# One list order for a whole attention and MLP program, and half of its scores as three single-pass products

## The chip, the cores and the metric

The kernel runs on one core of a Trainium2 chip. The time is device microseconds of one execution on that core, from the start of the program to its end; runs are repeated and the median is given.

## The reference

Four images (B = 4) of 448 positions go through three stages, all in fp32:

```python
# 1. attention with a soft cap, 12 heads of 64
scores = cap * np.tanh(scale * q @ k.T / cap)
x = softmax(scores) @ v                       # -> (4, 448, 768)
# 2. experts: 4, each a causal attention with head size 64; a position uses its two best
for e in range(4):
    ye = softmax(causal(scale * (x @ wq[e]) @ (x @ wk[e]).T)) @ (x @ wv[e]) @ wo[e]
    out += w[e] * ye                          # w: softmax over the two best gates, else 0
# 3. gated MLP
h = gelu_tanh(out @ w_in)                     # 1024 wide
u, v = h[..., :512], h[..., 512:]
gated = u * (w_sg @ layer_norm(v) * g_ln + b_sg)
return out + gated @ w_out
```

## The kernel before, in words

The first stage works on 24 pairs of heads, six to an image, a pair's two heads on the two row halves of the array (64 partitions each). Scores are made with keys on the partitions: three blocks of 128 keys and a tail of 64 to a pair (`block`, L440, and `tails`, L446; one tail tile serves two pairs). A block is two fp32 products, one per head, of 64x128 weights with 448 columns. Each goes to a PSUM tile `s` of which there are two; ScalarE frees it by Tanh and then runs Exp on two blocks at a time (`scores`, L455). `add_up` (L481) adds the blocks for the softmax's sums on VectorE (some of these additions are GpSimd's), `sums` (L516) forms the sums over the keys on TensorE, and `values` (L487) multiplies with v, whose result `po` ScalarE copies to `os`. The inverse sums of an image go through DRAM (`rd`, `ri`, `rb`), then `os` is multiplied by them and split into two fp32r parts, xh and xl, for the experts.

The second stage makes its products as three fp32r products of two-part operands (high by high, high by low, low by high): `queries_keys` (L670, tile `qk`), values (`v`), the attention (`a`), transposes (`tr`, `turn`, L769) and `attend`. It runs for one image while the attention of the next goes on, and is spread over the slots.

Before the first image is done, TensorE also makes a combined weight w2 from wo and w_in (tiles `w2ps`, in `prepare_weights`, L941); its two parts go to DRAM, and four loads of 512 KB in slots 12 to 15 (`W2_LOADS`) bring them back for the MLP.

Three things set the order. The function `slot` (L550) is written out by hand: slot i holds pair i's scores, pair i - 1's values, the loads for pair i + 2, and at the places "a", "w", "p" and "n" pieces of the experts' work, of the weights and of the loads. Slots 0 to 9 are the program's first part, 10 to 24 its second. Engines keep the order in which the program is written (`InOrder`, L328), but loads and stores are placed by the tile framework. The rest, the last image's experts and the MLP, is the third part: there `agenda.on` is set, each instruction is recorded by `Agenda.add` (L103), and `Agenda.order` (L166) puts them into a list: of what is ready by a model of durations and buffers, the instruction with the longest way to the end (its level) goes first. SP's transfers are in that list too.

Of the kernel before, what the change touches and what calls it, by code (L numbers as in the profile page):

```python
# [22 lines left out]
HP = H // 2  # L23
# [54 lines left out]
class Agenda:  # L78
# [5 lines left out]
    def __init__(self, tc, since):  # L84
        self.tc, self.since = tc, since
        self.ops, self.on = [], False
        self.seen, self.uses, self.caps = {}, {}, {}
        self.behind, self.fill = {}, tuple(f"{t}{b}" for t in "ov" for b in range(B))
# [14 lines left out]
    def add(self, eng, f, args, kw):  # L103
# [9 lines left out]
        for x, wr in [(x, False) for x in ins] + [(x, True) for x in outs]:  # L113
            t = x.tensor
            lo, hi, p0, p1 = self.span(x)
            for j, l, h, q0, q1, w in self.seen.setdefault(t.name, []):
                if (wr or w) and lo < h and l < hi and p0 < q1 and q0 < p1 and j != i:
                    after.add(j)
            if t.name not in self.uses:
                self.uses[t.name] = []  # L120
                if x.space != bass.MemoryType.DRAM and getattr(t, "tag", None) is not None:
                    self.caps.setdefault(t.cap_key, []).append((t.name, wr, t))
            self.uses[t.name].append(i)
            tiles.append(t.name)
# [5 lines left out]
        op = dict(i=i, eng=eng, call=lambda: f(*args, **kw), after=after, tiles=set(tiles), took=[], port=False)  # L130
# [3 lines left out]
        if eng == "pe":  # L134
            st, mv = (args[1], args[1]) if name == "transpose" else (kw.get("lhsT", args[1]), kw.get("rhs", args[-1]))
            n = mv.free_size() if name != "transpose" else args[1].partition_size()
            op["dur"] = (96.0 if name == "transpose" else .446 * n + 3.5 if st.dtype == F32R else 2 * max(.825 * n, 185.0))
# [8 lines left out]
        elif eng == "dve":  # L146
            op["dur"] = 150.0 + 1.04 * n
            if name == "tensor_tensor_reduce":
                op["dur"] += 165.0
            elif name == "reciprocal":  # L150
                op["dur"] = 150.0 + 6.3 * n
            elif name in ("tensor_scalar", "tensor_copy") and not psum:
                op["dur"] = 150.0 + .54 * n + (110.0 if n > 8 and any(x.free_size() == 1 for x in ins) else 0.0)
            op["port"] = not psum and n > 8
        elif eng == "pool":
            op["dur"] = 100.0 + 2.4 * n if len(big) > 1 else 600.0 + .25 * n
            op["port"] = name != "memset"
        else:
            op["dur"] = 450.0
            size = outs[0].partition_size() * outs[0].free_size() * 4 if outs[0].space != bass.MemoryType.DRAM else (  # L160
                ins[0].partition_size() * ins[0].free_size() * 4)
            op["bytes"] = size
            op["extra"] = 1500.0 if outs[0].tensor.name.startswith(("rb", "ri", "rd", "wo", "gln")) else 0.0
        self.ops.append(op)

    def order(self):  # L166
        ops, n = self.ops, len(self.ops)
        then = [[] for _ in ops]
        for op in ops:
            for j in op["after"]:  # L170
                then[j].append(op["i"])
        level = [0.0] * n
        for i in reversed(range(n)):
            op = ops[i]
            took = op["dur"] + self.LATENCY[op["eng"]]
            if op["eng"] == "sp":
# [3 lines left out]
            level[i] = took + max((level[j] for j in then[i]), default=0.0)  # L180
        slots, queue, where, left = {}, {}, {}, {t: len(set(u)) for t, u in self.uses.items()}
        for key, tiles in self.caps.items():
            cap = tiles[0][2].tag_meta.bufs
            old = [t for t, w, _ in tiles if not w]
            slots[key] = [0.0] * (cap - len(old)) + [None] * len(old)
            queue[key] = [t for t, w, _ in tiles if w]
            for t, w, _ in tiles:
                where[t] = (key, len(slots[key]) - 1 - old.index(t) if not w else None)
        need, ready, end = [len(op["after"]) for op in ops], [0.0] * n, [0.0] * n
        for op in ops:  # L190
            for t in op["tiles"]:
                for k, v in self.since.items():
                    if t.startswith(k) and where.get(t, (0, 0))[1] is not None:
                        ready[op["i"]] = max(ready[op["i"]], v)
        open_ = {}
        for t, u in self.uses.items():
            made = {i for i in u if ops[i]["eng"] == "pe" and ops[i]["bank"] == t}
            open_[t] = {j for i in made for j in ops[i]["after"] if ops[j]["eng"] != "pe"} or ({-1} if not made else set())
        feeds = [[] for _ in ops]
        for t, js in open_.items():  # L200
            for j in js - {-1}:
                feeds[j].append(t)
        free = dict.fromkeys(self.LATENCY, 0.0)
        pools = {e: [] for e in free}
        for op in ops:
            if not need[op["i"]]:
                pools[op["eng"]].append(op["i"])
        grid, cfg, bank, lock, pipe, done = [[0.0] * 4 for _ in range(4)], None, None, 0.0, 0.0, []

        def begin(i):  # L210
            op = ops[i]
            t = max(free[op["eng"]], ready[i])
            for x in op["tiles"]:
                key, s = where.get(x, (None, 0))
                if s is not None:
                    continue
                if queue[key][0] != x and (not x.startswith(self.fill) or open_[x] or sum(s is not None for s in slots[key]) < 2):
                    return None
                got = [s for s in slots[key] if s is not None]
                if not got:  # L220
                    return None
                t = max(t, min(got) + 60.0)
            if op["eng"] == "pe":
                r, c, r0, c0 = op["cell"]
                if (r, c) != cfg and cfg:
                    t = max(t, max(map(max, grid)) + (95.0 if (r, c) != cfg else 0.0))
                else:
                    t = max(t, max(grid[y][x] for y in range(r0, r0 + r) for x in range(c0, c0 + c)))
            if op["port"]:
                t = max(t, lock)  # L230
            return t

        while len(done) < n:
            best = None
            for e, pool in pools.items():
# [6 lines left out]
                if e == "pe":  # L242
                    t, i = max(near, key=lambda x: (ops[x[1]]["bank"] == bank, level[x[1]], -x[1]))
                elif e == "sp":
                    t, i = min(near, key=lambda x: x[1])
                else:
                    t, i = max(near, key=lambda x: (level[x[1]], -x[1]))
                if best is None or t < best[0]:
# [6 lines left out]
            for x in op["tiles"]:  # L255
                key, s = where.get(x, (None, 0))
                if s is not None:
# [6 lines left out]
            if e == "pe":  # L264
# [4 lines left out]
                cfg, bank = (r, c), op["bank"]  # L269
                free[e], end[i] = t + 7.0, t + op["dur"]  # L270
            elif e == "sp":
                pipe = max(pipe, t + 1950.0) + op["bytes"] / 330.0
                free[e], end[i] = t + op["dur"], pipe + op["extra"]
            else:
                end[i] = t + op["dur"]
                free[e] = end[i] - self.OVERLAP[e]
                if op["port"]:
                    lock = max(lock, end[i] - 60.0)
            op["at"] = t
            done.append(i)  # L280
            for x in feeds[i]:
                open_[x].discard(i)
            for j in then[i]:
                lat = 0.0 if ops[j]["eng"] == e != "sp" else self.LATENCY[e]
                ready[j] = max(ready[j], end[i] + lat)
# [3 lines left out]
            for x in op["tiles"]:  # L289
                left[x] -= 1  # L290
                if not left[x] and x in where:
                    key, s = where[x]
                    slots[key][s] = max(end[j] for j in self.uses[x])
        return sorted(range(n), key=lambda i: (ops[i]["at"], i))

    def run(self):
        self.on = False
        last = {}
        for i in self.order():
            op = self.ops[i]  # L300
            ins = op["call"]()
            for key in op["took"]:
                before = last.get(key)
                if before is not None and before.ins.engine != ins.ins.engine:
                    self.tc.add_manual_dep(ins.ins, before.ins.name, NOSYNC, reason="order")
                last[key] = ins


def build(ctx: ExitStack, tc: tile.TileContext, a: dict):
# [35 lines left out]
    agenda = Agenda(tc, {"pe": 2300.0, "rd": 2700.0})  # L345
# [109 lines left out]
    def scores(b, hp, h, qp, kp, then=None):  # L455
# [4 lines left out]
        for c2 in range(n):  # L460
            s = ps_s.tile([128, 2, 512], F32, tag="s", name=f"s{b}_{hp}_{2 * h + c2}")
            if 2 * h + c2 < KB:
                block(s, 2 * h + c2, qp, kp)
# [86 lines left out]
    def slot(i, side):  # L550
# [6 lines left out]
        if i + 2 < len(pairs):  # L557
# [4 lines left out]
            ld[i + 2] = qk  # L562
        if i < len(pairs):
# [188 lines left out]
    def settle(b, ep):  # L752

        for el in range(2):
# [4 lines left out]
            for i in range(NC):  # L759
                pe = PES[b, ep, el, i]  # L760
                by = "apavaaap"[4 * el + i] if agenda.on else "p"
# [86 lines left out]
    W2_LOADS = (12, 13, 14, 15)  # L848
# [4 lines left out]
    def beside(n):  # L853
# [4 lines left out]
        def side(place):  # L858
# [10 lines left out]
            else:  # L869
# [135 lines left out]
    with tc.tile_pool(name="pre", bufs=2) as pre:  # L1005
# [13 lines left out]
    w2 = ES(tc.tile_pool(name="w2", bufs=1, reuse_waits="tile"))  # L1019
    w2_t = [w2.tile([128, 2, FF], F32R, name=f"w2_{t}") for t in "hl"]  # L1020
    w2_h, w2_l = w2_t
    YA = {}
    for n in range(PRE_SLOTS, B * HP + 1):
        slot(n, beside(n))
    ah.close()
    agenda.on = True
# [7 lines left out]
    ml = ES(tc.tile_pool(name="ml", bufs=1, side="right", reuse_waits="tile"))  # L1034
    ps = ES(tc.tile_pool(name="ps", bufs=5, space=PSUM, side="right", reuse_waits="tile"))
# [7 lines left out]
    wo_l = wp.tile([128, 2, DM], F32R, name="wo_l", tag="wb")  # L1043

# [3 lines left out]
    def mlp_weights(part):  # L1048
# [176 lines left out]
    agenda.run()  # L1225
# [56 lines left out]
```

## Time and profile before

| | us |
|---|---|
| median of 3 runs | 509.02 (508.78 to 509.1) |
| the profiled execution, its own time | 510.37 |
| its span, first to last instruction | 508.6 |
| TensorE busy, 2702 products | 496.8 (98%) |
| VectorE, ScalarE, GpSimd busy | 330.8, 329.0, 94.2 |

The span is cut into stages by what runs: scores alone to 20 us, scores with the preparation of weights to 100, scores with the experts of the image before to 265, the last experts and the first MLP work to 370, and the MLP to the end. A row's name is `out<-in` with the buffer numbers left out: `s<-qp,kp` is a score product of queries and keys, and w2_h and w2_l are printed as `w_h` and `w_l`. `x8` counts instructions; an fp32 product counts as two. All recorded operations share line L338, so tiles tell them apart. [...]

### The profile page before, as it was taken

The numbers are of one execution on the slowest core, as the hardware profiler recorded it, in microseconds if no ns is written. First come the engines' busy times: TensorE is split into PE (matmuls) and PEld (weight loads), VectorE is DVE, ScalarE is ACT, GpSimd is POOL, SyncE is SP. The second block draws the span as 40 slices with busy tenths as digits, with TensorE's granted clock in tenths as the row PEclk, the third lists the DMA queues.
The fourth block names the chain that finished last, engine by engine and source line by source line (L and its number), as shares of the span: only waits on it lengthen the run. The fifth ranks groups of instructions, "written<-read, shape, count | busy, mean of one in ns | idle before, by whom it ended". The sixth has DMA issues, their size and how long they took to land.

```text
span 508.6 us, 7515 instructions
## 1 busy us (share of the span) xinstructions
PE 496.8 (98%) x2702; PEld 329.6 (65%) x2702; DVE 330.8 (65%) x719; ACT 329.0 (65%) x558; POOL 94.2 (19%) x103
## 2 busy tenths in 40 slices
PE   7999999999999999999999989999999999999997
PEld 2233333455555556655559777877799899989996
DVE  4899998992666664655664999847860594497050
ACT  6989989868788686678765757757831263355131
POOL 0000000133145152235063302031410010010000
PEclk9999999999999999999999999999999999999999
DMA  8974626885334142414023622015011001100212
GB/s 292 310 267 141 216 88 141 241 295 176 102 102 151 58 129 63 127 58 113 1 68 88 193 60 64 1 46 233 1 37 54 19 1 56 54 0 1 90 43 85
DMA packets 35188, 54.27 MB, mean 107 GB/s; under 512 B 5584, under 2 KB 30160, under 8 KB 35152
## 3 DMA queue, kind: packets, MB, share of 16 engines
q1 hardware_dynamic: 35008, 53.57, 33.4%
q8 instruction: 21, 0.34, 0.3%
q10 hardware_dynamic: 144, 0.23, 0.2%
q14 instruction: 15, 0.12, 0.1%
HBM read 42.04 MB, written 11.75 MB: 106 GB/s over the span
## 4 chain that ended last, share of the span: by engine, by line
PE 72%; DVE 12%; ACT 7%; DMA 4%; SPq 2%; issue 2%; POOL 0%; DVEq 0%; ACTq 0%; POOLq 0%
PE o L338 17%; PE s L338 8%; PE qk L338 8%; PE po L338 8%; PE sp L338 7%; PE v L338 6%; ACT p L338 4%; PE hu L338 3%; DVE pb L338 3%; PE a L338 3%; PE av L338 3%; PE tr L338 2%; DMA rb<-rd 2%; PE hv L338 2%; ACT pe L338 2%
## 5 line engine op out<-in xcount | busy, mean ns | idle before, releaser
L338 ACT ACTIVATE p<-s,tsc 128x896 f32<-128x896 f32 x84 | 80.9, 1006 | 20.3 <-PE s L338 20.0
L338 PE MATMUL s<-qp,kp 64*128 64x448 f32 (+1 forms) x384 | 79.1, 573 | 3.0 <-ACT p L338 3.0
L338 ACT ACTIVATE p<-p,capt 128x1792 f32<-128x1792 f32 (+1 forms) x48 | 77.0, 1603 | 1.1
L338 DVE TENSOR_TENSOR pb<-pb,p 128x896 f32<-128x896 f32 (+1 forms) x48 | 53.2, 1109 | 20.0 <-ACT p L338 10.7
L338 POOL TENSOR_TENSOR pb<-p 128x896 f32<-128x896 f32 x14 | 29.9, 2134 | 166.5 <-PE po L338 94.7
L338 PE MATMUL po<-p,vv 128*64 128x448 f32 x288 | 59.4, 548 | 0.0
L338 PEld LDWEIGHTS s<-qp,kp 64*128 64x128 f32 (+1 forms) x384 | 27.7, 176 | 48.4 <-issue 23.5
L338 ACT ACTIVATE ob<-o 128x448 f32<-128x448 f32 x24 | 12.9, 544 | 53.1 <-PE o L338 49.0
L338 DVE SCALAR_TENSOR_TENSOR vs<-sp,gln,bsg 128x448 f32<-128x448 f32 x16 | 10.6, 680 | 54.9 <-PE sp L338 54.7
L338 PEld LDWEIGHTS po<-p,vv 128*64 128x64 f32 x288 | 18.5, 136 | 37.9 <-issue 34.1
L338 DVE CUSTOM_DVE_ANT_0 a<-a,neg 112x112 f32<-112x112 f32 (+3 forms) x64 | 27.7, 468 | 20.8 <-PE a L338 20.2
L338 ACT ACTIVATE pe<-a,m 112x112 f32<-112x112 f32 (+3 forms) x64 | 31.1, 493 | 11.5 <-DVE m L338 11.5
L338 PE MATMUL qk<-xh,wqk_h 128*128 128x448 f32 x96 | 37.6, 391 | 0.1
L338 PE MATMUL o<-gh,wu_l 128*128 128x448 f32 x96 | 35.0, 365 | 0.0
L338 PE MATMUL o<-gl,wu_h 128*128 128x448 f32 x96 | 35.0, 364 | 0.0
L338 PE MATMUL qk<-xh,wqk_l 128*128 128x448 f32 x96 | 35.0, 364 | 0.0
L338 PE MATMUL o<-gh,wu_h 128*128 128x448 f32 x96 | 34.9, 364 | 0.0
L338 POOL TENSOR_TENSOR rstd<-rstd,mhalf 128x1 f32<-128x1 f32 (+1 forms) x16 | 10.8, 678 | 121.1 <-DVE rstd L338 119.2
L338 POOL TENSOR_SCALAR pe<-pe,cs 112x224 f32<-112x224 f32 (+3 forms) x40 | 24.1, 621 | 45.7 <-DVE cs L338 44.6
L338 PE MATMUL v<-wvg_h,xh 128*112 128x260 f32 x96 | 28.2, 294 | 1.4 <-ACT pe L338 1.3
L338 PE MATMUL v<-wvg_h,xl 128*112 128x260 f32 x96 | 27.1, 283 | 0.0
L338 PE MATMUL v<-wvg_l,xh 128*112 128x260 f32 x96 | 27.1, 282 | 0.0
(237 smaller groups left out, 1083.8 us busy)
## 6 DMA issues: line engine op xcount, KB each, us to landing
rb<-rd SPq DMA_DIRECT2D x24, 224.0 KB, 5.4
out_dram<-ob SPq DMA_DIRECT2D x24, 224.0 KB, 1.9
kp<-in_kT_dram SPq DMA_DIRECT2D x23, 224.0 KB, 3.0
qp<-in_qT_dram SPq DMA_DIRECT2D x23, 224.0 KB, 3.3
vv<-in_v_dram SPq DMA_DIRECT2D x24, 192.0 KB, 3.3
wuw<-in_w_out_dram SPq DMA_DIRECT2D x5, 384.0 KB, 5.0
wud<-wuw SPq DMA_DIRECT2D x10, 192.0 KB, 1.9
ws<-in_wqk_dram SPq DMA_DIRECT2D x4, 384.0 KB, 7.9
```

The source lines that it names most:

```text
L338: return tc.keep_in_program_order(f(*args, **kw))
```

## The change

All three parts are now recorded and ordered by the list scheduler. Parts one and two are keyed by the place in the program (`rank`) and not by the level; the state of engines, buffers and the array goes over from part to part. Products that lie side by side in the array start as one (`gang`). Loads and stores of all three parts are in the list. From pair 12 on, `part` rounds q and k to fp32r on ScalarE (qh, kh) and subtracts on VectorE (ql, kl), one slot ahead, and `block` makes three fp32r products for a head instead of one fp32 product; tails stay as they were. The loads of w2 leave slots 12 to 15 and its pool, and are the first transfers of part three, in a pool of their own.

```diff
-    def order(self):
+    def order(self, new, by_level, floor):
...
-            level[i] = took + max((level[j] for j in then[i]), default=0.0)
+            op["level"] = took + max((ops[j]["level"] for j in then[i]), default=0.0)
+            op["key"] = op["level"] if by_level else -op["rank"]
...
+        gang, team = {}, []
+        for i in new:
+            op = ops[i]
+            if op["eng"] != "pe":
+                continue
+            r, c, r0, c0 = op["cell"]
+            if (r, c) == (4, 4) or not team or (r, c) != ops[team[0]]["cell"][:2] or any(
+                    abs(r0 - ops[j]["cell"][2]) < r and abs(c0 - ops[j]["cell"][3]) < c for j in team):
+                team = []
+            team.append(i)
+            gang[i] = team
...
-                    t, i = max(near, key=lambda x: (ops[x[1]]["bank"] == bank, level[x[1]], -x[1]))
+                    t, i = max(near, key=lambda x: (ops[x[1]]["bank"] == self.bank, ops[x[1]]["key"], -x[1]))
...
-    def block(s, c, qp, kp):
-
-        for j in range(2):
-            r = slice(64 * j, 64 * j + 64)
-            mm(s[:, j, :S], kp[r, c * 128:(c + 1) * 128], qp[r, :], start=True, stop=True)
+    PARTED = 12
+
+    parts = {}
+
+    def part(i):
+
+        if PARTED <= i < len(pairs):
+            parts[i] = []
+            for x, t, h, l in zip(ld[i], "qk", 'aa', 'vv'):
+                xh, xl = (at.tile([128, S], F32R, tag=t + p, name=f"{t}{p}{i}", bufs=2) for p in "hl")
+                rnd(h, xh, x[:, :S])
+                rest(l, xl, x[:, :S], xh)
+                parts[i].append((xh, xl))
+
+    def block(s, c, qp, kp, i):
+
+        q, k = parts.get(i, ((qp,), (kp,)))
+        of = [(k[0], q[0]), (k[0], q[-1]), (k[-1], q[0])][:1 if len(q) == 1 else 3]
+        for n, (y, x) in enumerate(of):
+            for j in range(2):
+                r = slice(64 * j, 64 * j + 64)
+                mm(s[:, j, :S], y[r, c * 128:(c + 1) * 128], x[r, :], start=(n == 0), stop=(n == len(of) - 1))
...
             ld[i + 2] = qk
+        part(i + 1)
         if i < len(pairs):
...
-                if place == "n" and n in W2_LOADS:
-                    t, k = divmod(W2_LOADS.index(n), 2)
-                    dma(w2_t[t][:, k, :].bitcast(F32), w2_d[t][:, k, :])
...
+        agenda.on = True
+        agenda.free["pe"] = 3400.0
         for n in range(PRE_SLOTS):
             slot(n, beside_pre(n))
+        agenda.run(False, )
+        used = max(op["end"] for op in agenda.ops)
...
+    agenda.on = True
     for n in range(PRE_SLOTS, B * HP + 1):
         slot(n, beside(n))
+    agenda.run(False, lambda key: used if str(key).split("_")[-2] in ("mo", "ypool", "w2") else 0.0)
...
+        for k in range(2):
+            for t, w in enumerate((w2_h, w2_l)):
+                dma(w[:, k, :].bitcast(F32), w2_d[t][:, k, :])
         dve.memset(mhalf, -0.5)
...
-    agenda.run()
+    agenda.run(True, lambda key: closed if str(key).split("_")[-2] in ("ml", "w4", "mr", "ps") else 0.0)
```

In the orders that follow a name's last number is the tile's own. The first place is TensorE at the start, from the tail of pair (0,0)'s scores on; s0_1_0 is block 0 of pair (0,1), po0_0 the values of pair (0,0). Before:

```order
L338 MATMUL s0_0_3_172<-qp0_1_125,kp0_1_126 64x448 x2
L338 MATMUL s0_1_0_186<-qp0_1_125,kp0_1_126 128x448 x2
L338 MATMUL s0_1_1_190<-qp0_1_125,kp0_1_126 128x448 x2
L338 MATMUL po0_0_208<-p0_0_0_135,vv0_0_121 64x448 x4
L338 MATMUL po0_0_208<-p0_0_1_167,vv0_0_121 64x448 x2
L338 MATMUL s0_1_2_220<-qp0_1_125,kp0_1_126 128x448 x2
L338 MATMUL s0_2_0_232<-qp2_131,kp2_132 128x448 x2
L338 MATMUL s0_2_1_236<-qp2_131,kp2_132 128x448 x2
```

After:

```order
L387 MATMUL s0_0_3_130<-qp0_1_114,kp0_1_115 64x448 x2
L387 MATMUL po0_0_140<-p0_0_0_119,vv0_0_112 64x448 x4
L387 MATMUL s0_1_0_134<-qp0_1_114,kp0_1_115 128x448 x2
L387 MATMUL s0_1_1_135<-qp0_1_114,kp0_1_115 128x448 x2
L387 MATMUL po0_0_140<-p0_0_1_128,vv0_0_112 64x448 x2
L387 MATMUL po0_0_140<-p0_0_1_128,vt0_0_113 64x448 x2
L387 MATMUL po0_1_155<-p0_0_1_128,vt0_0_113 64x448 x2
L387 MATMUL s0_1_2_144<-qp0_1_114,kp0_1_115 128x448 x2
L387 MATMUL s0_2_0_148<-qp2_117,kp2_118 128x448 x2
L387 MATMUL w2ps0_0_161<-wi0m_122,wt_108 128x512
L387 MATMUL po0_1_155<-p0_1_0_133,vv0_1_116 64x448 x4
L387 MATMUL s0_2_1_149<-qp2_117,kp2_118 128x448 x2
```

Four products of po0_0 now stand ahead of s0_1_0, and w2ps0_0 stands ahead of s0_2_1. The second place is TensorE at pair (2,3), whose blocks are s2_3_0 and following; sum2_0 are the sums of image 2's first two pairs, and tr0 are transposes of image 0's experts. Before:

```order
L338 MATMUL sum2_0_1306<-pb2_0_972,onehot_71 32x448 x2
L338 MATMUL sum2_0_1306<-pb2_1_1097,onehot_71 32x448 x2
L338 MATMUL s2_3_0_1332<-qp15_1068,kp15_1069 128x448 x2
L338 MATMUL s2_3_1_1336<-qp15_1068,kp15_1069 128x448 x2
L338 MATMUL po2_2_1348<-p2_2_0_1207,vv2_2_1111 64x448 x4
L338 MATMUL po2_2_1348<-p2_2_1_1255,vv2_2_1111 64x448 x2
L338 MATMUL s2_3_2_1360<-qp15_1068,kp15_1069 128x448 x2
```

After:

```order
L387 MATMUL tr0_0_0_2_920<-ident_73,pe0_0_0_2_871 112x112 x3
L387 MATMUL s2_3_0_931<-qh15_900,kh15_902 128x448 x2
L387 MATMUL s2_3_0_931<-ql15_901,kh15_902 128x448 x2
L387 MATMUL s2_3_0_931<-qh15_900,kl15_903 128x448 x2
L387 MATMUL s2_3_1_932<-qh15_900,kh15_902 128x448 x2
L387 MATMUL s2_3_1_932<-ql15_901,kh15_902 128x448 x2
L387 MATMUL s2_3_1_932<-qh15_900,kl15_903 128x448 x2
L387 MATMUL tr0_0_0_3_921<-ident_73,pe0_0_0_3_883 112x112 x4
L387 MATMUL sum2_0_922<-pb2_0_841,onehot_71 32x448 x2
L387 MATMUL sum2_0_922<-pb2_1_876,onehot_71 32x448 x2
L387 MATMUL po2_2_935<-p2_2_0_904,vv2_2_878 64x448 x4
```

A block is three rows, and the scores stand between two runs of transposes, with the sums behind them. The third place is ScalarE at pair (1,4), the slot in which pair 12 is rounded: p1_4 are that pair's Tanhs (from s) and Exps (from p), kh12 and qh12 the roundings. Before:

```order
L338 ACTIVATE wvg_h_78<-ws9_726 128x780
L338 ACTIVATE p1_4_0_798<-s1_4_0_799,tsc_70 128x2x448
L338 ACTIVATE p1_4_0_798<-s1_4_1_803,tsc_70 128x2x448
L338 ACTIVATE p1_4_0_798<-p1_4_0_798,capt_69 128x1792
L338 ACTIVATE os1_3_818<-po1_2_734 128x448
L338 ACTIVATE os1_3_818<-po1_3_813 128x448
L338 ACTIVATE p1_4_1_829<-s1_4_2_830,tsc_70 128x2x448
```

After:

```order
L387 ACTIVATE p1_4_0_791<-s1_4_0_792,tsc_70 128x2x448
L387 ACTIVATE os1_3_797<-po1_2_282 128x448
L387 ACTIVATE kh12_811<-kp12_790 128x448
L387 ACTIVATE qh12_809<-qp12_789 128x448
L387 ACTIVATE os1_3_797<-po1_3_796 128x448
L387 ACTIVATE p1_4_0_791<-s1_4_1_793,tsc_70 128x2x448
L387 ACTIVATE p1_4_1_799<-s1_4_2_800,tsc_70 128x2x448
```

Both roundings and a copy of os stand between the Tanhs of s1_4_0 and s1_4_1.

## Rows read from the trace of the kernel before

**Rows 1.** Windows by stage: engine busy time (x instructions), granted clock, DMA share, GB/s.
```profile
0.00:20.00 20.00, 15.75 (x66) 5.37 (x66) 11.11 (x22) 14.99 (x14) 1.12 (x6) 1.00 0.89 298
20.00:100.00 80.00, 79.94 (x372) 27.55 (x368) 73.20 (x103) 72.47 (x79) 2.08 (x1) 1.00 0.63 191
100.00:265.00 165.00, 163.35 (x984) 91.31 (x988) 101.27 (x225) 122.80 (x190) 58.13 (x56) 1.00 0.37 113
265.00:370.00 105.00, 102.65 (x632) 82.45 (x625) 80.19 (x244) 70.83 (x190) 26.52 (x33) 1.00 0.26 84
370.00:508.60 138.60, 135.13 (x657) 122.88 (x656) 64.98 (x129) 47.90 (x88) 6.40 (x9) 1.00 0.11 40
...
120.00:265.00 145.00, 143.49 (x884) 81.27 (x880) 84.73 (x200) 108.03 (x171) 49.80 (x52) 1.00 0.31 91
```

**Rows 2.** Waits of TensorE: us in total, times, longest.
```profile
PE s L338 <- ACT p L338: 3.0, 3, 1.4
```

**Rows 3.** The chain of waits: start us, us, what, by pieces.
```profile
27.39 1.70 PE s L338 x8
...
31.50 0.95 PE s L338 x4
...
109.31 3.84 PE qk L338 x18
...
375.51 18.33 PE o L338 x90
```

**Rows 4.** TensorE timeline at the start: start us, us, what, [idle before <- releaser].
```profile
8.43 1.28 PE L338 MATMUL s<-qp,kp 64*64 64x448 f32 x8 [0.32 <-ACT p L338]
11.15 1.92 PE L338 MATMUL s<-qp,kp 64*128 64x448 f32 x8 [1.44 <-ACT p L338]
...
18.38 1.02 PE L338 MATMUL s<-qp,kp 64*128 64x448 f32 x4 [1.20 <-ACT p L338]
```

**Rows 5.** ScalarE timeline at the start.
```profile
8.41 1.79 ACT L338 ACTIVATE p<-p,capt 128x1792 f32<-128x1792 f32 x1
...
23.35 0.96 ACT L338 ACTIVATE os<-po 128x448 f32<-128x448 f32 x2
```

**Rows 6.** TensorE timeline around sum1_1.
```profile
102.28 1.98 PE L338 MATMUL sum<-pb,onehot 128*32 128x448 f32 x8
```

**Rows 7.** VectorE timeline around the same place.
```profile
96.90 2.44 DVE L338 TENSOR_TENSOR os<-os,rb 128x896 f32<-128x896 f32 x1 [0.85 <-DMA rb<-rd]
...
101.04 2.21 DVE L338 TENSOR_TENSOR pb<-pb,p 128x896 f32<-128x896 f32 x2
```

**Rows 8.** TensorE timeline, transposes of the expert attention.
```profile
195.42 0.47 PE L338 MATMUL tr<-ident,pe 112*112 112x112 f32 x3 [0.45 <-ACT vp L338]
...
205.49 0.47 PE L338 MATMUL tr<-ident,pe 112*112 112x112 f32 x3 [0.33 <-ACT pe L338]
```

**Rows 9.** Groups by form: busy us, mean ns of one, idle before and releasers.
```profile
L338 ACT ACTIVATE p<-s,tsc 128x896 f32<-128x896 f32 x84 | 80.9, 1006 | 20.3 <-PE s L338 20.0 <-DVE pb L338 0.2
...
L338 PEld LDWEIGHTS qk<-xh,wqk_h 128*128 128x128 f32 x96 | 18.0, 188 | 10.2 <-issue 4.1 <-ACT pe L338 1.9 <-ACT y L338 1.3
...
L338 DVE TENSOR_TENSOR gl<-vs,gh 128x448 fp32r<-128x448 f32 x16 | 9.8, 621 | 1.8 <-ACT gh L338 1.3
...
L338 ACT ACTIVATE gh<-vs 128x448 fp32r<-128x448 f32 x16 | 9.0, 577 | 5.8 <-DVE vs L338 5.8
```

**Rows 10.** SP's issues at the head of the last part.
```profile
266.32 0.33 SPq L351 DMA_DIRECT2D rd<-rs  x1
```

**Rows 11.** TensorE timeline around the head of the last part.
```profile
264.65 0.96 PE L338 MATMUL sum<-pb,onehot 128*32 128x448 f32 x8
...
276.48 0.48 PE L338 MATMUL hv<-w_h,yh 128*128 128x512 f32 x1
```

**Rows 12.** Tile w2_l, its loads from DRAM.
```profile
L351 SPq DMA_DIRECT2D w_l<-w2d x2: 327/692/1057, 104.6 to 105.5; - x2
...
DMA to landing us min/median/max: 4.7/5.9/7.1
```

More of the change, by code (lines that the diff above doesn't have):

```diff
@@ L82, with __init__ @@
     OVERLAP = {"act": 100.0, "dve": 80.0, "pool": 27.0, "sp": 0.0}
-    def __init__(self, tc, since):
-        self.tc, self.since = tc, since
-        self.ops, self.on = [], False
+    def __init__(self, tc):
+        self.tc = tc
+        self.ops, self.on, self.late, self.end = [], False, 0, False
         self.seen, self.uses, self.caps = {}, {}, {}
-        self.behind, self.fill = {}, tuple(f"{t}{b}" for t in "ov" for b in range(B))
+        self.behind, self.fill = {}, ()
+        self.slots, self.queue, self.where, self.left = {}, {}, {}, {}
+        self.free = dict.fromkeys(self.LATENCY, 0.0)
+        self.grid = [[0.0] * 4 for _ in range(4)]
+        self.cfg = self.bank = None
+        self.lock = self.pipe = 0.0
+        self.last, self.kept = {}, set()
     def hold(self, these, those):
@@ new lines, in order @@
+        slots, queue, where, left = self.slots, self.queue, self.where, self.left
+        keep = {t for tiles in self.caps.values() for t, _, _ in tiles[-tiles[0][2].tag_meta.bufs:]}
+        for t, u in uses.items():
+            left[t] = len({i for i in u if "end" not in ops[i]}) + (t in keep)
+            if t in self.kept and not left[t] and where.get(t, (0, None))[1] is not None:
+                key, s = where[t]
+                slots[key][s] = max(ops[j]["end"] for j in u)
+        self.kept = keep
@@ new lines, in order @@
+        for key, tiles in self.caps.items():
+            fresh = [(t, w) for t, w, _ in tiles if t not in where]
+            old = [t for t, w in fresh if not w]
+            if key not in slots:
+                slots[key] = [floor(key)] * tiles[0][2].tag_meta.bufs
+                queue[key] = []
+            for t in old:
+                s = next((s for s, v in enumerate(slots[key]) if v is not None), None)
+                where[t] = (key, s)
+                if s is not None:
+                    slots[key][s] = None
+            for t, w in fresh:
+                if w:
+                    queue[key].append(t)
+                    where[t] = (key, None)
@@ L197, in order @@
+        need, ready = {}, {}
+        for i in new:
+            need[i] = sum("end" not in ops[j] for j in ops[i]["after"])
+            ready[i] = max([0.0] + [self.past(j, i) for j in ops[i]["after"] if "end" in ops[j]])
+        open_, feeds = {}, {i: [] for i in new}
+        for t, u in uses.items():
             made = {i for i in u if ops[i]["eng"] == "pe" and ops[i]["bank"] == t}
-            open_[t] = {j for i in made for j in ops[i]["after"] if ops[j]["eng"] != "pe"} or ({-1} if not made else set())
@@ L208, in order @@
-        grid, cfg, bank, lock, pipe, done = [[0.0] * 4 for _ in range(4)], None, None, 0.0, 0.0, []
+        for i in new:
+            if not need[i]:
+                pools[ops[i]["eng"]].append(i)
+        gang, team = {}, []
+        for i in new:
+            op = ops[i]
[7 more added lines that the diff above has]
+            gang[i] = team
@@ L210, in begin @@
         def begin(i):
             op = ops[i]
-            t = max(free[op["eng"]], ready[i])
-            for x in op["tiles"]:
+            t, mates, new_tiles = free[op["eng"]], [i], {}
+            if i in gang and gang[i][0] == i:
+                mates = gang[i]
+                if any("end" not in ops[q] for j in mates for q in ops[j]["after"] if q not in mates):
+                    return None
+                t = max([t] + [self.past(q, j) for j in mates for q in ops[j]["after"] if q not in mates])
@@ L227, in begin @@
+                got = sorted(s for s in slots[key] if s is not None)
+                if len(got) <= n:
+                    return None
+                t = max(t, got[n] + 60.0)
+                mine.append(x)
+            for j in mates if op["eng"] == "pe" else ():
+                r, c, r0, c0 = ops[j]["cell"]
+                if (r, c) != self.cfg and self.cfg:
+                    t = max(t, max(map(max, grid)) + 95.0)
                 else:
@@ L462, in scores @@
             if 2 * h + c2 < KB:
[L463 removed]
+                block(s, 2 * h + c2, qp, kp, b * HP + hp)
             else:
```

151 lines of the change are left out of this document (69 added, 82 removed).

## The prediction

> **What bounds the kernel now.** I read the profile in five views. [...] VectorE and ScalarE have room from 120 us on: busy 84.73 and 108.03 of 145. [...] Second, TensorE's waits [rows 2]: 3.0 us for Tanh in three pieces, all at the start. Third, the chain of waits [rows 3], which gives TensorE's work by the block, and last, timelines of single places.
>
> **The change part by part.**
>
> **Score products.** Pairs 12 to 23 have three whole blocks of 128 keys each, 36 in all; their tails stay fp32. The chain shows two fp32 blocks in a run of 1.70 us and one alone in 0.95 [rows 3]: a block is 1.70 - 0.95 = 0.75 us and entering a run costs 0.95 - 0.75 = 0.20. A block is two products, on the two row halves of the array, side by side. Now each half gets three fp32r products over the same 448 columns. The steady fp32r product of the last stage takes 18.33 / 90 = 0.204 us [rows 3]; that is on the whole array, and no row shows fp32r on a half. If the halves run side by side as the fp32 ones do, a block is 3 x 0.204 = 0.61 us, 0.14 less: 36 x 0.14 = **5.0 us gained**. Bounds: a quarter of the fp32 block is 0.187; at that step the gain is 36 x (0.75 - 0.56) = 6.7. If the halves do not run side by side, six steps are 1.22, and 36 x 0.47 = 17 us are lost. I take 0.204: the same data type and the same width, and the fp32 halves of this very shape already run together.
> [...]
>
> **Entries into runs.** Whenever the array's tile shape changes, TensorE pays an entry: 0.20 us above, and 3.84 - 18 x 0.204 = 0.17 for the eighteen projection products at 109.31 [rows 3]. I counted the runs of one tile shape in both orders: 163 before, 177 after; up to pair (1,4) 49 and 51, from there to the score blocks' end 78 and 91, behind that 36 and 35. In the order shown for pair (2,3) a transpose run and a sums run have changed places around the scores. 14 x 0.17 to 0.20 = 2.4 to 2.8, **2.7 us lost**.
>
> **The start.** TensorE waits 0.32 us at 8.43, 1.44 at 11.15 and 1.20 at 18.38 for Tanh to empty one of the two score buffers [rows 4]; these three are the waits of [rows 2]. After, the first four value products stand ahead of s0_1_0 (order at the start); their input is ready when the first Exp ends, 8.41 + 1.79 = 10.20, just inside the wait, and an expert weight's product stands between later score blocks. So part of 1.44 + 1.20 = 2.64 us fills. But ScalarE runs from 8.41 to 24 without a gap [rows 5], so its Tanhs come no sooner; work done inside the wait is saved only where later waits don't grow. I take **1.5 gained**, bounds 0 and 2.6.
>
> **Waits for VectorE's sums and for transposes.** sum1_1 runs 1.98 us at 102.28 [rows 6] where a sums run is 0.96 at 264.65 [rows 11]: about 1.0 of wait, since the additions to pb stand behind the division of os, 2.44 us from 96.90 [rows 7]. In the new VectorE order only the last and shortest of pair (1,3)'s additions is left behind that division, and it stands right behind it: about 99.4 + 1.1 = 100.5, before the sums start. Transposes wait 0.45 at 195.42 and 0.33 at 205.49 [rows 8]. 1.8 in all at most; I take **0.8 gained**, bounds 0 and 1.8.
>
> **Roundings.** ScalarE gets 24 of 577 ns and VectorE 24 subtractions of 621 ns, taken from the same operations at 128x448 in the last part [rows 9]: 13.8 and 14.9 us. They lie in 120 to 265, where ScalarE is free for 145 - 108 = 37 us and VectorE for 60 [rows 1]. Taken at **0**; if the cover is gone it is the second rival. A pair's rounding stands in the slot before its scores, so its q and k must be there about one slot earlier; they are asked for two slots ahead, as before.
>
> **Weights of the MLP.** The four 512 KB loads of w2 leave slots 12 to 15 and go to the head of the last part on SP, in its new order two ahead of the store rd3 and two behind it. rd3 is issued at 266.32 [rows 10], the first product that reads w2 starts at 276.48 [rows 11], and loads of that size landed in 4.7 to 7.1 us [rows 12]: 267.3 + 7.1 = 274.4, 2 us early. Two issues ahead of rd3 delay it by under a microsecond, and SP has nothing queued there that TensorE waits for before 276. **0**. If a load were late, up to 2 us of the first MLP products would slip.
>
> **New waits.** The list in the last part knows durations only by a model. In 265 to 370, already ordered so, TensorE idles 2.35 of 105 [rows 1]; in the hand-ordered 20 to 265, 1.71 of 245. If the list idled there at its own rate, 2.35 / 105 x 245 = 5.5 us minus what is left of the old 1.71. But the first two parts are keyed by the program's order, not by level, so most of the hand order stands; GpSimd, whose work is the same and which is busy 49.80 of 145 [rows 1], keeps its slack. I take **0.8 lost**, bounds 0 and 5.5.
>
> Sum: -5.0 + 2.7 - 1.5 - 0.8 + 0.8 = -3.8 us. The profiled execution took 510.37 (span 508.6), so 506.6; the median of the runs, 509.02, lies 1.35 under it, hence **505.2**.
>
> **The rivals.**
> *More than that* (0.14): step 0.187 (-6.7), start -2.6, waits -1.8, entries +2.4, no new waits: -8.7, 500.3. [...] Against: the fp32r products in the rows run at 0.204.
> *Nothing to see* (0.10): new waits of 3 to 5 us eat the gain; 508 to 510.
> *Slower, by ScalarE* (0.16). Only two score buffers exist, and each is freed by a Tanh of 1.006 us [rows 9]. kh12 and qh12 stand back to back between the two Tanhs of pair (1,4) (order on ScalarE); two roundings are 1.15 us there. If TensorE waits it out at every pair, 12 x 1.15 = 13.8 lost, at half of them 6.9: 505.2 + 6.9 = 512.1. It decides from 3.8 / 12 = 0.32 us a pair on. For it: that order, and the start, where TensorE waits for just this. Against: behind 20 us TensorE never waited for a Tanh [rows 2, 4], with ScalarE at 75% from 120 on, and later pairs spread the two roundings.
> *The three products don't overlap* (0.06): the halves run one after the other, or each product waits for its weights. A weight load is 0.188 [rows 9] and 0.204 + 0.188 = 0.39 a step makes a block 1.18, 36 x 0.43 = 15 lost: 520 or more. Against it: eighteen projection products, each with its load on the same rows of the array, took 3.84 us, not 7.
> [...]
>
> **How the numbers follow.** Forecast 0.54, 503 to 507.5. Together with "more" 0.68 faster by over 0.2% (1.0 us, about what a measurement of this kernel tells from no change), 0.10 within it, 0.16 + 0.06 = 0.22 slower. The range 499.5 to 512.5 takes in the first three cases and half of the ScalarE rival, and leaves out the rest of that (0.08), the last (0.06) and a little below.
>
> **What would show it.** Score blocks of three products at about 0.61 us in a run; TensorE busy some 2 us less in all (5.0 - 2.7); idle before 20 us down from 4.25 to about 2.8; no row "PE s <- ACT" behind 120 us; hv's first product not waiting for a load. Wrong would be: a score step near 0.39, waits on Tanh or on ScalarE's roundings from pair 12 on, or idle time from 20 to 265 over 5 us.

## The result and the profile after

The changed kernel takes 512.40 us (median of 7 runs, 510.07 to 513.18) against 509.02 (7 runs, 508.30 to 510.48): a ratio of 1.0059, interval [1.0038, 1.0080]. It is slower by 0.6% where 505.2 was forecast. The profiled execution is the quickest of the seven, 510.07 with a span of 508.2, so its trace shows less than the median loses. The mean granted clock differs from run to run, 0.992 to 0.997; that of the kernel before is 0.999 or 1.00.

Windows by stage of the changed kernel, to be held against [rows 1]. The columns are the stage's length, the busy time of TensorE, of its weight loads, of VectorE, ScalarE and GpSimd (x instructions), the granted clock, the DMA share and GB/s:

```profile
0.00:20.00 20.00, 18.10 (x76) 5.69 (x76) 12.63 (x25) 15.99 (x17) 1.12 (x6) 1.00 0.93 328
20.00:100.00 80.00, 77.50 (x362) 27.31 (x361) 68.70 (x103) 68.93 (x76) 0.00 (x0) 1.00 0.63 193
100.00:265.00 165.00, 164.01 (x1096) 102.35 (x1095) 121.75 (x253) 135.60 (x219) 71.67 (x61) 1.00 0.35 104
265.00:370.00 105.00, 101.14 (x599) 79.06 (x598) 75.41 (x228) 67.14 (x181) 21.04 (x26) 0.98 0.27 90
370.00:508.20 138.20, 134.10 (x649) 121.07 (x647) 67.91 (x136) 49.47 (x92) 7.78 (x10) 1.00 0.11 41
```

TensorE's idle time moved: 1.90 us of the first 20 (4.25 before), but 2.50 from 20 to 100 (0.06) and 3.86 from 265 to 370 (2.35), and there the clock is 0.98. The chain of waits shows the score blocks, as [rows 3] do:

```profile
145.51 1.43 PE s L387 x12
...
150.76 0.80 PE s L387 x6
```

A block is 1.43 - 0.80 = 0.63 us, forecast 0.61. TensorE is busy 494.8 us, 2.0 less than before. Some 1.7 of it is only there because the clock is at 0.50 for 3.4 us in this execution (windows of 304 to 310 us below), so at full clock it would be an estimated 3.7 less. The score products do what was forecast. TensorE's timeline has two waits that were not there, at 98.53 and 304.12:

```profile
98.53 1.08 PE L387 MATMUL s<-qp,kp 64*64 64x448 f32 x8 [2.50 <-ACT p L387]
```

```profile
299.02 0.45 PE L387 MATMUL hu<-yh,w_h 128*128 128x448 f32 x1
...
300.40 0.83 PE L387 MATMUL a<-qk 64*112 64x112 f32 x8
301.17 0.50 PE L387 MATMUL tr<-ident,pe 112*112 112x112 f32 x3
304.12 1.09 PE L387 MATMUL tr<-ident,pe 112*112 112x112 f32 x7 [2.45 <-ACT pe L387]
```

Matching both timelines by the program's order gives the starts of the same products (us):

| first product of | before | after | difference |
|---|---|---|---|
| sum0_0 | 26.43 | 24.69 | -1.74 |
| qk0_0_0 (needs image 0's xh) | 98.05 | 94.14 | -3.91 |
| s1_5_0 | 104.18 | 102.65 | -1.53 |
| sum3_2 (end of part two) | 264.65 | 259.58 | -5.07 |
| hv0_0 (first to read w2) | 276.48 | 271.61 | -4.87 |
| av2_1 | 330.97 | 329.35 | -1.62 |
| o1_0 | 402.48 | 400.84 | -1.64 |

So the first two parts gain 5 us, the size that was forecast, and the third part, of which the prediction moved nothing but four loads, gives 3.4 of it back before 331 us and most of the rest in the tail. Some 0.3 us of the lead belongs to the profiled execution of before: `w2_blind` (below), which has the same order on TensorE, starts sum0_0 at 26.17 and sum3_2 at 264.38.

### The profile page after: what moved, and what is told of

It reads as the page before. It is cut to its first block, busy times and chain, and to the rows that moved or that the text cites. A ratio compares the mean times of both kernels' runs of the same rounds, so it can differ in the third digit from the quotient of the medians.

```text
span 508.2 us, 7748 instructions
## 1 busy us (share of the span) xinstructions
PE 494.8 (97%) x2774; PEld 335.5 (66%) x2774; DVE 346.4 (68%) x743; ACT 337.1 (66%) x582; POOL 101.6 (20%) x103
## 4 chain that ended last, share of the span: by engine, by line
PE 87%; DVE 5%; ACT 4%; DMA 3%; issue 1%; POOL 0%; ACTq 0%; DVEq 0%; SPq 0%; POOLq 0%
PE o L387 17%; PE po L387 13%; PE s L387 12%; PE qk L387 10%; PE sp L387 6%; PE v L387 5%; PE w2ps L387 4%; PE hv L387 4%; PE a L387 4%; PE hu L387 3%; PE av L387 3%; PE tr L387 3%; ACT p L387 2%; PE sum L387 2%; DMA wuw<-in_w_out_dram 1%; DMA qp<-in_qT_dram 1%
## 5 line engine op out<-in xcount | busy, mean ns | idle before, releaser
L387 ACT ACTIVATE p<-s,tsc 128x896 f32<-128x896 f32 x84 | 82.9, 1010 | 15.6 <-PE s L387 13.1
L387 PE MATMUL s<-qp,kp 64*128 64x448 f32 (+1 forms) x240 | 46.0, 569 | 2.9 <-ACT p L387 2.9
L387 PEld LDWEIGHTS s<-qp,kp 64*128 64x128 f32 (+1 forms) x240 | 15.0, 166 | 30.4 <-issue 12.4
L387 POOL TENSOR_SCALAR pe<-pe,cs 112x224 f32<-112x224 f32 (+3 forms) x40 | 28.3, 723 | 30.5 <-DVE cs L387 30.1
```

The costliest lines, as they stand in the source:

```text
L387: return tc.keep_in_program_order(f(*args, **kw))
```

## The experiments

Each kernel is held against runs of the kernel before that were made along with it; their medians are 509.05 to 509.31.

**The changed kernel once more, and without the products.** `again` is unedited; `list_only` has `PARTED = 24` in place of 12.

> The changed kernel, unedited. Theory A (the last part loses what the first two gain): 510 to 513 us, the last part's first product (sum3_2) some 5 us earlier than before and the end within 1 us of before's. Theory B (waits of 2.5 us let TensorE's clock fall, and how much differs from run to run): runs spread over 3 us, and the longer ones show a mean granted clock of about 0.992 instead of 0.997, with a second or a longer stretch at 0.5. If the clock doesn't follow the time, B falls.

> The list order in all three parts, but every score product stays fp32 and nothing is rounded. Theory C (the roundings, waiting for loads ahead of Tanhs on ScalarE, make the 2.5 us wait at 98.5): that wait is gone, sum3_2 starts 264.65 - 2.4 (start) + some entries, 262 to 264. Rival (the list itself makes the wait, roundings or not): a wait of over 2 us on Tanh near 98 stays. In all, with 5.0 us of score gain missing: 512 to 515 us if the last part loses 4 us as in the changed kernel.

Measured: 511.20 us (12 runs, 510.08 to 515.00, ratio 1.0049 [1.0028, 1.0070]), and 516.14 (5 runs, 1.0140 [1.0118, 1.0163]). The difference is what the products are worth under the list order: 4.9 us, where 36 blocks were forecast at 5.0. `list_only` is over the 512 to 515 expected. Without the products the list's order gains nothing in the first two parts: in its profile sum3_2 starts at 267.78, 3.1 later than before, behind the wait shown next and 3.4 us at half clock. `list_only` has no wait on Tanh at 98, so theory C looked right; but another wait stands nearly in its place, for VectorE's xh:

```profile
101.00 0.47 PE L387 MATMUL qk<-xh,wqk_h 128*128 128x448 f32 x1 [3.24 <-DVE xh L387]
```

Theory B stands. The runs of `again` follow the clock: 510.08 to 511.40 us at 0.995 to 0.997, 512.37 to 513.75 at 0.993, 514.59 at 0.989, 515.00 at 0.987. Its profile and that of the first run are two executions of one kernel with the same two waits. Here it is the first wait (2.53 us, before 98.7) after which the clock falls, and not the second. Windows of `again` (columns as in the stages above):

```profile
98.70:100.00 1.30, 1.30 (x9) 0.59 (x10) 1.26 (x2) 1.30 (x2) 0.00 (x0) 0.96 0.61 236
100.00:102.00 2.00, 2.00 (x7) 1.75 (x7) 0.03 (x1) 2.00 (x3) 0.71 (x1) 0.50 0.61 186
102.00:104.00 2.00, 2.00 (x13) 1.11 (x11) 0.00 (x0) 2.00 (x3) 1.40 (x1) 0.67 0.12 44
...
306.00:308.00 2.00, 1.98 (x13) 1.08 (x13) 2.00 (x9) 1.47 (x6) 0.00 (x0) 1.00 0.02 4
```

In the first profile of the changed kernel it is the other way round:

```profile
98.50:100.00 1.50, 1.47 (x10) 0.75 (x11) 0.73 (x1) 1.50 (x2) 0.00 (x0) 1.00 0.33 131
100.00:104.00 4.00, 4.00 (x26) 2.19 (x24) 1.19 (x2) 4.00 (x4) 2.12 (x1) 1.00 0.38 119
...
304.00:306.00 2.00, 1.86 (x11) 1.25 (x11) 2.00 (x11) 1.78 (x7) 0.00 (x0) 0.79 0.01 4
306.00:308.00 2.00, 2.00 (x8) 0.53 (x6) 1.80 (x8) 1.39 (x4) 0.00 (x0) 0.50 0.19 66
308.00:310.00 2.00, 2.00 (x16) 1.07 (x14) 1.18 (x5) 0.64 (x3) 1.12 (x2) 0.86 0.00 0
```

From qk0_0_0 to s1_5_0 the one takes 10.10 us and the other 8.51: this fall costs 1.6 us on top of its wait. Theory A stands too: in the profile of `again` sum3_2 starts at 261.30, so the lead is 3.35 us where the clock has fallen before it, and at the end 0.3 us are left, without a fall in the last part.

**What the last part loses by.** `w2_late` is the kernel before with the loads of w2 at the head of part three and nothing else. In `w2_blind` they are issued past the list:

```diff
+    for k in range(2):
+        for t, w in enumerate((w2_h, w2_l)):
+            sp.engine.dma_start(w[:, k, :].bitcast(F32), w2_d[t][:, k, :])
...
-        for k in range(2):
-            for t, w in enumerate((w2_h, w2_l)):
-                dma(w[:, k, :].bitcast(F32), w2_d[t][:, k, :])
```

> The kernel before with one edit: the four loads of w2 at the head of the last part. Theory A1 (these loads push the conversion loads and VectorE's chain of the last part about): 1 to 4 us slower than before, with a new wait over 2 us of TensorE between 280 and 310. Theory A2 (the last part loses by the list's other new rules): within 0.5 us of before.

> The kernel before with w2's four loads at the head of the last part, as in w2_late, but the list scheduler doesn't see them: on TensorE, VectorE, ScalarE and GpSimd every instruction stands as in the kernel before, and only SP's queue differs. Theory A1a (it is the new order of the last part that cost w2_late 4.7 us, not the traffic): 508.5 to 509.5 us, clock 0.999 or more. Theory A1b (the 2 MB themselves hold up the inverse sums and conversions): 512 to 515 us, as w2_late, with waits over 1 us near 300.

Measured: `w2_late` 513.78 us (12 runs, 509.49 to 516.93, 1.0079 [1.0051, 1.0107]); `w2_blind` 509.12 (12 runs, 1.0000 [0.9991, 1.0009]). The same 2 MB at the same place on SP cost nothing; that the list knows of them costs 4.7 us, because it then writes another order. Most of the 4.7 goes with the clock: three runs of `w2_late`, at 0.999 or 1.00, took 509.49 to 510.27 us, and the nine at 0.990 to 0.997 took 511.99 to 516.93. In the profile of `w2_late` TensorE waits twice near 300, neither time for the 2 us that theory A1 expected, and the clock falls there to 0.50:

```profile
298.82 1.00 PE L338 MATMUL a<-qk 64*112 64x336 f32 x2 [1.23 <-ACT pt L338]
301.49 1.01 PE L338 MATMUL av<-pt,vp 112*64 112x448 f32 x2 [1.66 <-ACT pe L338]
```

```profile
299.00:301.50 2.50, 0.84 (x4) 0.10 (x3) 2.50 (x6) 1.21 (x4) 0.55 (x1) 0.56 0.21 62
301.50:303.00 1.50, 1.50 (x4) 0.51 (x6) 1.50 (x5) 1.01 (x4) 0.00 (x0) 0.50 0.00 0
```

`after_blind` makes the same edit to the changed kernel.

> The changed kernel, with w2's four loads issued at the same place on SP but unseen by its list. Theory A1a, that w2 in the list makes the last part's order bad: 505 to 507 us and no wait over 1.5 us near 304. Theory A2, that the list's other new rules do it: 510.5 to 512 as the changed kernel, with the wait of 2.4 us.

Measured: 507.75 us (12 runs, 506.24 to 510.47, 0.9982 [0.9967, 0.9996]), 3.5 less than `again` and 0.25 over the upper end of theory A1a, with no wait over 0.5 us between 265 and 330. On TensorE only twelve products and the rows they pass have moved: hu0_0 stands behind v3, not ahead of it, and hu0_1 between two transpose runs, just where the changed kernel waits at 304.12:

```profile
298.60 1.51 PE L387 MATMUL a<-qk 64*112 64x112 f32 x8
300.04 0.50 PE L387 MATMUL tr<-ident,pe 112*112 112x112 f32 x3
300.31 0.45 PE L387 MATMUL hu<-yh,w_h 128*128 128x448 f32 x1
...
301.40 0.37 PE L387 MATMUL hu<-yh,w_l 128*128 128x448 f32 x1
301.77 1.08 PE L387 MATMUL tr<-ident,pe 112*112 112x112 f32 x7
```

So six of these products, 1.2 us (a row takes 0.36 to 0.45, but the starts are 0.20 to 0.28 apart), now cover the softmax between the two runs; the list with w2 in it spent them earlier. They are not the whole of the 2.45 us: the products of `a` ahead of the first run take 1.51 us in place of 0.83, and from their start to the second run it is 3.17 us in place of 3.72, where VectorE's and ScalarE's orders have changed too. The clock has its share here as well: six of the twelve runs show 0.999 (506.24 to 507.31 us) and six 0.996 or 0.997 (508.19 to 510.47), while no run of `again` is above 0.997.

**The last part in its old order.** `old_part3` gives part three to the list as it was (its class from the kernel before); `old3_blind` also hides w2 from it:

```diff
-    agenda.on = agenda.end = True
-    agenda.fill = tuple(f"{t}{b}" for t in "ov" for b in range(B))
+    agenda = OldAgenda(tc, {"pe": 2300.0, "rd": 2700.0})
+    agenda.on = agenda.end = True
...
-    agenda.run(True, lambda key: closed if str(key).split("_")[-2] in ("ml", "w4", "mr", "ps") else 0.0)
+    agenda.run()
```

> The changed kernel, but the last part is ordered by the list scheduler as it was before (its old rules and old start state), with w2's loads still at its head. Theory A2: the lead of 5 us at sum3_2 is kept to the end, 503.5 to 505.5 us, clock over 0.997. Theory A1 (the loads are to blame): 508 to 512, as the changed kernel.

> The first two parts as in the changed kernel, wait at 98.5 included; the last part by the old rules with w2 unseen, in the order of the kernel before. If the last part's order alone took the gain away: the lead of 3.4 to 5.0 us at sum3_2 stays, 504 to 506 us.

Measured: 509.63 us (12 runs, 1.0005 [0.9988, 1.0022]) and 506.25 (5 runs, 505.93 to 507.36, 0.9951 [0.9939, 0.9963]). With the old rules, too, the list loses by knowing of the loads: 3.4 us. `old3_blind` beats both kernels; it is 0.25 over the 504 to 506 expected. From sum3_2 on, going by the names in the two traces, all 372 of VectorE's rows stand in the order of the kernel before and 1276 of TensorE's 1288 (235 and 1154 in the changed kernel); its sum3_2 starts 5.40 us early and o1_0 still 3.98.

**The products in the hand order.** `hand_parts_blind` is the kernel before with `part`, the new `block` and w2 past the list; every other instruction of VectorE, ScalarE and GpSimd stands as before.

> The kernel before in its hand order, with the three-product scores from pair 12 on and w2's loads late and unseen by the list: the products alone. The prediction's term: 36 blocks at 0.14 us less, 5.0 us: 504 to 504.5 us if w2_blind is as before. Rival (the roundings on ScalarE hold the score buffers in the hand order): 506 to 512, with waits on Tanh behind 100 us. Rival (the traffic of w2 costs): 508 to 510.

Measured: 516.65 us (4 runs, 1.0152 [1.0137, 1.0168]), 7.5 slower and slower than all three expected. Where two blocks stand in one run the products' own gain is there (the chain has `s x12` at 1.42), and more than it is lost. Of the waits of TensorE:

```profile
PE a L338 <- ACT pe L338: 1.7, 2, 1.1
...
PE tr L338 <- ACT vp L338: 1.1, 1, 1.1
PE po L338 <- ACT pe L338: 1.1, 1, 1.1
```

VectorE's timeline shows how the first of them, 1.15 us at 118.20, comes about: a pair's two subtractions stand ahead of the expert attention's maximum (a), which ScalarE's Exp (pe) and all behind it wait for (ScalarE idles 1.53 us to 117.70). These two take 1.32 and 1.42 us, where the next pair's take 0.61 each (129.28 and 129.82).

```profile
112.33 2.39 DVE L338 TENSOR_TENSOR pb<-pb,p 128x896 f32<-128x896 f32 x2
114.75 1.32 DVE L338 TENSOR_TENSOR ql<-qp,qh 128x448 fp32r<-128x448 f32 x1
115.99 1.42 DVE L338 TENSOR_TENSOR kl<-kp,kh 128x448 fp32r<-128x448 f32 x1
117.34 0.27 DVE L338 CUSTOM_DVE_ANT_0 a<-a,neg 112x112 f32<-112x112 f32 x1
```

The same order stands ahead of the wait of 1.06 us at 166.22; what makes up the rest of the 7.5 us is not shown. For Tanh a score product waits once behind 100 us, 0.38 us at 142.86. VectorE's idle time elsewhere (6.95 us before 126.61) covered nothing for what stood behind the two; of the two orders, only the list's makes these products pay. A hand order with the subtractions further back was not run.

**The wait at 98.5.** In the changed kernel ScalarE's rounding of kh12 waits for its load with the Tanhs queued behind it:

```profile
95.93 0.58 ACT L387 ACTIVATE kh<-kp 128x448 fp32r<-128x448 f32 x1 [3.81 <-DMA kp<-in_kT_dram]
96.57 0.58 ACT L387 ACTIVATE qh<-qp 128x448 fp32r<-128x448 f32 x1
97.05 0.53 ACT L387 ACTIVATE os<-po 128x448 f32<-128x448 f32 x1
97.47 1.90 ACT L387 ACTIVATE p<-s,tsc 128x896 f32<-128x896 f32 x2
```

`late_loads` adds 4000 ns in the model to every load of queries and keys, `late12` to those of pairs 12 to 23 alone; `best` and `best2` are the two on top of `old3_blind`.

```diff
-            op["extra"] = 1500.0 if outs[0].tensor.name.startswith(("rb", "ri", "rd", "wo", "gln")) else 0.0
+            op["extra"] = 1500.0 if outs[0].tensor.name.startswith(("rb", "ri", "rd", "wo", "gln")) else (
+                4000.0 if outs[0].tensor.name.startswith(tuple(f"{t}{i}" for t in ("qp", "kp") for i in range(12, 24))) else 0.0)
```

> The changed kernel, with one edit in the list's model: a load of queries or keys is taken to land 4 us later. On ScalarE kh12 and qh12 then stand behind the Tanhs of pair (1,4). Theory C (a rounding that waits for its load holds the Tanhs behind it): the 2.5 us wait at 98.5 is gone, 508 to 509.5 us, and a clock fall near 100 us goes with it. If the wait only moves to the next rounding: 510.5 to 512.

> The first two parts as in the changed kernel with late_loads' edit; the last part by the list's old rules, with w2's loads unseen by it, so in the order of the kernel before. If all three theories hold: the lead of 5 us at sum3_2 plus 2 us, kept to the end: 501.5 to 503.5 us, clock 0.999 or more. If the last part loses by a shifted start alone, whatever its order: 506 to 509.

> The changed kernel; in the list's model the loads of queries and keys of pairs 12 to 23 alone land 4 us later. All that moves are rows of ScalarE: qh12 and kh12 now stand behind the Tanhs of s1_4_1, s1_4_2 and s1_4_3, and the next pair's two change places with a Tanh and an Exp; TensorE, VectorE and GpSimd keep their order. Theory C (a rounding that waits for its load holds the Tanhs behind it): the 2.5 us wait at 98.5 shrinks under 0.5, 508.5 to 509.5 us. If the wait moves on to the products that need qh12, 510.5 to 511.5.

> Both edits: late12's on ScalarE and the last part in the order of the kernel before. If both theories hold and add: old3_blind less 2 us, 502 to 504 us, clock 0.999 or more.

Measured: `late_loads` 519.68 us (5 runs, 1.0216 [1.0194, 1.0238]) and `best` 514.04 (4 runs, 1.0100 [1.0085, 1.0115]). Their misses say nothing of kh12: the first pairs' loads were put late too, and TensorE waits 4.5 us at 11.5. `late12` has that mended: 513.19 us (6 runs, 1.0078 [1.0059, 1.0096]), 2.0 above `again`; `best2` 508.10 (12 runs, 0.9984 [0.9975, 0.9994]), 1.9 above `old3_blind`; both were expected to gain. The wait on Tanh is gone as theory C says, and TensorE runs into the next one, longer, for VectorE's last piece of xh; below, that piece and GpSimd's work at the time:

```profile
100.74 0.74 PE L388 MATMUL qk<-xh,wqk_h 128*128 128x448 f32 x1 [3.69 <-DVE xh L388]
```

```profile
98.30 2.39 DVE L388 CAST xh<-os 128x896 fp32r<-128x896 f32 x1
```

```profile
97.29 2.92 POOL L388 TENSOR_TENSOR pb<-p 128x896 f32<-128x896 f32 x1 [95.64 <-ACT p L388]
```

The cast takes 2.39 us (2.40 in `best2`, 2.39 in `list_only`) where it takes 0.63 in the first profile of the changed kernel:

```profile
97.47 0.63 DVE L387 CAST xh<-os 128x896 fp32r<-128x896 f32 x1
```

```profile
101.14 2.12 POOL L387 TENSOR_TENSOR pb<-p 128x896 f32<-128x896 f32 x1 [99.48 <-ACT p L387]
```

There GpSimd's addition starts at 101.14, since kh12 had also held up the Exp that it adds (99.25 to 101.05 on ScalarE). So the rounding's wait kept the two apart. To test this (theory D), `best3` and `old3_dve` give that one addition to VectorE, on top of `best2` and `old3_blind`:

```diff
-            (dve if b == 0 or (b, hp) < (1, 4) else pool_e).tensor_tensor(pb, p[:, :, 0, :], p[:, :, 1, :], op=ALU.add)
+            (dve if b == 0 or (b, hp) < (1, 5) else pool_e).tensor_tensor(pb, p[:, :, 0, :], p[:, :, 1, :], op=ALU.add)
```

> best2 with one more edit: the first addition of pair (1,4)'s sums is VectorE's and not GpSimd's; it stands behind the last piece of xl. Theory D (GpSimd's addition at 98 is what stretches VectorE's xh from 0.63 to 2.4 us, and that is the wait that late12 and best2 ran into): the xh at 98.7 takes 0.7 us again, TensorE's wait at 101 falls from 3.3 to about 1.5, 505.5 to 506.5 us. Rival (the inverse sums' load rb sets that time, whatever GpSimd does): xh no earlier, 507.5 to 508.5.

> old3_blind with the same edit, the roundings' wait for their loads left in. There GpSimd's addition came late, at 101, and stretched nothing: theory D expects no gain from the edit, 506 to 507 us, and the 1.9 us wait on Tanh near 98 as in old3_blind.

Measured: `best3` 504.37 us (4 runs, 503.87 to 505.83, 0.9906 [0.9891, 0.9920]) and `old3_dve` 505.76 (6 runs, 505.35 to 508.32, 0.9946 [0.9925, 0.9967]). Both are under the times expected. Theory D holds. The edit gives 3.7 us where the two met and 0.5 where they did not, which the intervals do not tell from nothing; and with it theory C's edit gives 1.4. Of the 3.7 us, 2.1 are TensorE's wait for xh (3.31 in `best2`, 1.21 in `best3`), and the rest goes with the clock, 0.992 to 0.999 in the runs of `best2`. In `best3` the cast and TensorE's wait are

```profile
97.88 0.63 DVE L619 CAST xh<-os 128x896 fp32r<-128x896 f32 x1
```

```profile
98.57 0.47 PE L619 MATMUL qk<-xh,wqk_h 128*128 128x448 f32 x1 [1.21 <-DVE xh L619]
```

and the clock is 1.00 in each of its runs. It is the best of all, 0.9% under the kernel before: the change with four edits.

## Why the prediction was wrong

**Score products: right; entries: not measured alone.** 0.63 us a block (0.61 taken); 4.9 us between `list_only` and `again`. TensorE's busy time is 2.0 us less, where 5.0 - 2.7 = 2.3 was expected, but that they are so near is chance: 1.7 us of half clock are in it, and in `old3_blind`, whose profile is at full clock throughout, it is 4.5 less. Of these some 1.1 are the wait inside sum1_1 (1.98 before, 0.89 in the changed kernel). The halves do run side by side, and no product waits for its weights: 0.63 us a block leaves no room for either (1.22 and 1.18 by the prediction's sums). The rows' 0.204 held, 0.63 / 3 = 0.21 a step; no run shows the step of 0.187 that the "more" case is added up from.

**The start: gained more, then given back.** 1.74 us at sum0_0 and 3.9 at qk0_0_0, but 1.5 at s1_5_0: the roundings, and behind them image 0's xh, were not ready for it. That the pair's q and k are needed one slot earlier was in the text, "asked for two slots ahead, as before"; what stood behind the rounding on ScalarE while its load landed (6.4 us by the chain of waits, where the list's model takes 1.95 + 0.7) was not costed. **Waits for sums and transposes**: gone, as forecast; from 100 to 265 one wait over 0.2 us is left, 0.63 at 255.17, and the kernel before has it too (260.21). **New waits**: one of 2.5 us, within its bounds (0 to 5.5), not the 0.8 taken. With it the first two parts come out 5.1 early in the first profile, better than the 3.8 of the whole sum, and 3.35 early in `again`, where the clock falls behind that wait.

**"Weights of the MLP: 0" is the step that failed.** It looked at SP's queue and at the landing of the loads, and there it was right: the traffic costs nothing (`w2_blind`). It did not see that the loads had become entries of a list that orders the whole last part by a model, and that part was taken as unchanged. Hidden from the list they give back 3.5 us (`after_blind`), in the kernel before 4.7. Between `after_blind` and `old3_blind` lie another 1.5, for the list's other new rules and its carried state; but the runs at a clock of 0.999 or more took 506.24 to 507.31 us and 505.93 to 506.29, so without the clock it is nearer 0.6, and how much of the 1.5 these rules cost stays open. The orders of the last part could have been compared ahead; they were compared for the first two.

**The clock was missing from the sum.** In [rows 1] the clock is 1.00 in every stage, and the sum has no term for it. The mean over the 12 runs of `again` is 0.994; time lost at half clock is then an estimated (1 - 0.994) x 511 = 3 us, half of the 6.0 by which its median lies above 505.2. Two waits of about 2.5 us replaced several short ones. Each costs itself and, in a part of the executions, more at half the clock (1.6 us in the profile of `again`). So the sum against one profiled execution also failed as a scale: the changed kernel's is 2.3 us under its median, that of before 1.35 over. The "slower" side was forecast through the time of ScalarE's roundings, at every pair or every other one. It came about at one pair, (1,4), the place that the prediction named, and through the load that the rounding waited for (3.81 us), not the rounding's 0.58. In the hand order VectorE's subtractions did the harm. That the rival's 512.1 is close to the measured 512.40 is luck.

With part three left as it was and w2 unseen by its list, 506.25 was to be had, 1.0 above the forecast, and 504.37 with the wait at 98.5 mended and one addition moved. So the terms that the forecast costed were near what the runs showed, and it failed by the part that it took as unchanged and by the clock.

## What to carry to other kernels

A greedy list order is not local: one more entry can move every instruction behind it, so compare the whole new order, the "unchanged" part above all, and look there for products that used to cover a chain. Before you fix a wait, look for what it keeps apart: taking out a 2.5 us wait made this kernel slower until an addition that it had held back was moved too. Extra work on idle engines can still cost: under the list's order the products gained 4.9 us with it, but in the hand order two of the subtractions stood ahead of something that TensorE then waited 1.15 us for. So look at what stands behind such work in its engine's queue.

## What the runs showed of the hardware

Idle waits of 2.45 to 2.53 us of TensorE were followed by about 3.4 us at a granted clock of 0.50 in some executions and by full clock in others, for the same wait of the same kernel: the one that ends near 98.6 took 2.53 us in `again`, with a fall behind it, and 2.50 in the first profile, with 1.00 behind it. Waits of 1.20 and 1.44 us in the profile of before were not followed by a fall, nor were those of 1.88 and 2.11 us in the profiles of `old3_blind` and `after_blind`; but in `w2_late` the clock fell near 299.3, after a wait of 1.23 us and before the one of 1.66, and stayed at 0.50 to about 306. So in these profiles the length of one wait does not tell whether a fall follows.

A VectorE cast of 128x896 took 2.39 to 2.40 us instead of 0.63 beside an addition of GpSimd's, in three profiles (`late12`, `list_only`, `best2`), and 0.63 again with that addition gone (`best3`, `old3_dve`). In the profile of before all nine of these casts run with no GpSimd instruction beside them, in 0.62 to 0.63 us. In the first profile of the changed kernel seven do, in 0.61 to 0.63 us, and the two beside an addition, at 154.22 and 235.19, take 2.25 and 2.52. All five stretched casts end 0.48 to 0.49 us behind the addition beside them, whenever that ends (100.69 and 100.21 in `late12`, 156.47 and 155.99 in the changed kernel).
